# An S4 convolution woven into a SiLU feed-forward: first transform in 64-row halves, the outset in halves, the last step's loads ahead

## The chip, the cores and the metric

The kernel runs on one core of a Trainium2 chip. Its time is the device time of one execution in microseconds (us); several executions are timed, and their median is quoted. One further execution is recorded by the hardware profiler; all durations below come from it. TensorE is PE in the profile (its weight loads PEld), VectorE is DVE, ScalarE is ACT, GpSimd is POOL, and SyncE, which here only issues DMAs, is SP.

## The reference

One sequence of L = 2048 rows with D = 576 channels. Its normalised rows feed two branches, which are added to the input.

```python
xn = layernorm(x)
# branch A: a state-space convolution with N = 128 states a channel
dt = exp(log_dt)[:, None]; A = A_re + 1j*A_im
P  = exp((dt*A)[:, :, None] * arange(L))                 # D x N x L
K  = einsum("dn,dnl,dn->dl", C, P, dt*B).real            # the response
y  = irfft(rfft(pad(xn.T)) * rfft(pad(K)))[:, :L].T + xn * Dskip
# branch B: a feed-forward with F = 4608
out = silu(xn @ w1) @ w2
return x + y + out
```

All inputs and the output are float32.

## The kernel before, in words

**Feed-forward.** `ffn` works on 4 blocks of 512 rows, in two halves of two blocks, and on 9 chunks of 512 hidden units (FT = 4 tiles of 128). Each fp32 operand is split into a high and a low part of a shorter format (fp32r: `h1`, `l1`, `h2`, `l2`, `gh`, `gl`, `xh`, `xl`), and products are taken as high x high + high x low + low x high. `up(blk, t)` (line 255) makes one 128 x 512 tile of hidden units in PSUM with 14 matmuls, applies SiLU (line 268, `gf`), and splits the result on ScalarE (line 269, `gh`) and VectorE (line 270, `gl`). `down(blk, jj)` (line 273) multiplies the gate by w2 for one tile of 128 rows, in two column halves of 12 matmuls (line 285, `po`), and adds to `acc[j]` (line 288). `load_w1` and `load_w2` fetch two tiles of weights at a time into `w1r` and `w2r`, one buffer each, and split them (lines 236, 238, 249, 251).

**Rows.** `phase0` loads two tiles of 128 rows of x, normalises them (`norm`) and transposes them on PE (`put_xt`, lines 114 to 124) into `xh`, `xl`, `x4`. Tiles 0 to 7 are transposed before the woven part, in pool `pa`; tiles 8 to 15 during it, parked in DRAM (`dxt`). All normalised rows also go to DRAM (`dxn`).

**Convolution.** It is a transform of length 2048 by steps of 32 and 64. `spread` does the first step for the rows (line 145, `pu`) into DRAM `d1u`. `kgen` (line 427) makes the response 8 channels and two groups at a time, 36 chunks: sines and magnitudes on ScalarE and VectorE, then per pair of chunks 64 small matmuls over the states (line 530, `kp`, 128 x 32 weights, four column tiles). `kp` is copied to SBUF in two halves (line 539, `kt`), each half is multiplied by the constant `f1` (line 542, `z`: the response's first transform), and `z` is copied into `stage` (line 547), which is stored to DRAM `d1k` every four chunks. `spectral` (line 560) takes 32 frequencies one after another: loads `ur`, `kr`, splits them, second step (`pk`, `pu2`), product, inverse step (`pb`), and stores `yo` to DRAM `d2`. The last step is `add_conv(j, dst)` (line 631): it loads `ys`, 128 x 4 x 288, in two DMAs from `d2`, runs 8 matmuls with 64 rows and 32 columns (line 645, `py`), two row halves and four column tiles, and adds the result to `dst` (line 651). For tiles 8 to 15 `dst` is the accumulator, in `down` of the last chunk (line 278). Tiles 0 to 7 were finished in the first half and put into DRAM `dr0`; `tail` (line 603) reloads each as `r0`, calls `add_conv` and stores it.

**What sets the order.** `weave` (line 31) runs the feed-forward as the main line of 288 steps and resumes `side` when the step reaches a mark. `marks` (line 655) gives the places: response from 0.14 to 0.65, spectral part to 0.88, tail to 0.94. This gives a program order; a list scheduler with its own model of time then moves instructions on each engine, `tc.high_priority()` lifts those inside it, and `behind(ins)` keeps an instruction after another one. What results is a fixed order on each engine, and each engine and each DMA queue works through its own in order. SP's queue holds nearly all loads and stores; POOL's a few. Small PSUM tiles (`pt`, `pu`, `kp`, `z`, `pk`, `pb`, `py`) share three buffers (pool `pss`).

Of the kernel before, what the change touches and what calls it, by code (L numbers as in the profile page):

```python
# [17 lines left out]
P = 128  # L18
# [23 lines left out]
def kernel(  # L42
# [43 lines left out]
    ident = cst.tile([P, P], F32, name="ident")  # L86
    f1 = cst.tile([P, 2 * P], F32, name="f1")
    s4 = None
# [37 lines left out]
    xts = {}  # L126
    pins = {}

    def spread(up):
# [86 lines left out]

    def behind(ins):
        return tc.issue_after(ins) if ins is not None else nullcontext()

    def ffn():  # L220
# [4 lines left out]
        def load_w1(half, c, t):  # L225
            f = c * FT + t
            r1 = wp.tile([P, 5, 2 * P], F32, tag="w1r", name="w1r", bufs=1)
            fs = slice(f * P, (f + 2) * P)
            nc.sync.dma_start(r1[:, 0:4, :], w1[0:512, fs].rearrange("(k p) f -> p k f", p=P))
            nc.sync.dma_start(r1[0:64, 4, :], w1[512:576, fs])  # L230
            nc.sync.dma_start(r1[64:128, 4, :], w1[512:576, fs])
            for i in range(2):
                h1 = wp.tile([P, 5, P], F32R, tag="w1h", name="w1h", bufs=FT + 1)
                l1 = wp.tile([P, 5, P], F32R, tag="w1l", name="w1l", bufs=FT + 1)
                src = r1[:, :, i * P:(i + 1) * P]
                nc.scalar.copy(h1, src)  # L236
                with behind(pins["xt_v"] if f == half == 0 else None):
                    nc.vector.tensor_sub(l1, src, h1)  # L238
                W1[half, c, t + i] = h1, l1

        def load_w2(half, c, t):
            f = c * FT + t
            r2 = wp.tile([P, 2, D], F32, tag="w2r", name="w2r", bufs=1)
            nc.sync.dma_start(r2, w2v[:, f:f + 2, :])
            for i in range(2):
                h2 = wp.tile([P, D], F32R, tag="w2h", name="w2h", bufs=FT + 1)
                l2 = wp.tile([P, D], F32R, tag="w2l", name="w2l", bufs=FT + 1)
                with behind(pins["xt_s"] if f == half == 0 else None):
                    nc.scalar.copy(h2, r2[:, i, :])  # L249
                with behind(pins["xt_v"] if f == half == 0 else None):  # L250
                    nc.vector.tensor_sub(l2, r2[:, i, :], h2)  # L251
                W2[half, c, t + i] = h2, l2
                yield

        def up(blk, t):
            half, c, b = blk
            xh, xl, x4 = xts[2 * half + b]
            h1, l1 = W1[half, c, t]
            ph = ps1.tile([P, 512], F32, tag="ps1", name="ph")
# [3 lines left out]
            nc.tensor.matmul(ph, h1[:, 4, :], x4, start=False, stop=False)  # L263
            nc.tensor.matmul(ph, l1[:, 4, :], x4, start=False, stop=True)  # L264
            gf = gp.tile([P, 512], F32, tag="gf", name="gf", bufs=2)
            gh = gp.tile([P, 512], F32R, tag="gh", name="gh")
            gl = gp.tile([P, 512], F32R, tag="gl", name="gl")
# [3 lines left out]
            G[blk, t] = gh, gl  # L271

        def down(blk, jj):
            half, c, b = blk
            j = 8 * half + 4 * b + jj
            js = slice(jj * P, (jj + 1) * P)
            if half == 1 and c == NCH - 1:
                add_conv(j, acc[j])
            for h in range(2):
                hs = slice(h * HD, (h + 1) * HD)  # L280
                po = ps2.tile([P, 512], F32, tag="ps2", name="po")
                n = 0
                for t in range(FT):
                    for g, w in ((0, 0), (0, 1), (1, 0)):
                        nc.tensor.matmul(po[:, :HD], G[blk, t][g][:, js], W2[half, c, t][w][:, hs],  # L285
                                         start=n == 0, stop=n == 3 * FT - 1)
# [51 lines left out]

    kl = yp = None
    kf = {}  # L340
# [86 lines left out]
    def kgen():  # L427
        lrT, fT, rhoT, phiT = (kf[n] for n in ("lr", "f", "rho", "phi"))
        with tc.tile_pool(name="kg", bufs=1) as kg:
# [52 lines left out]
            for i in range(NCK):  # L482
# [52 lines left out]
                tabs = []  # L535
                for e in range(2):
                    es = slice(e * 256, (e + 1) * 256)
                    kt = kg.tile([P, 256], F32, tag="kt", name="kt", bufs=2)
                    nc.scalar.copy(kt, kp[:, es])
                    z = pss.tile([P, 512], F32, tag="pss", name="z")  # L540
                    for gl in range(2):
                        nc.tensor.matmul(z[:, gl * 256:(gl + 1) * 256], kt[:, gl * P:(gl + 1) * P], f1,  # L542
                                         start=True, stop=True)
                    r = (i - 1 + e) % NRUN
                    if r == 0:
                        stage = kg.tile([P, 64, NRUN * CH], F32, tag="stage", name="stage")
                    nc.scalar.copy(
                        stage[:, :, r * CH:(r + 1) * CH].rearrange("p k (g c) -> p g k c", g=2),
                        z.rearrange("p (g k c) -> p g k c", g=2, c=4))
                if r == NRUN - 1:  # L550
                    d0 = (i // NRUN) * NRUN * CH
# [51 lines left out]
    def tail():  # L603
        for j in range(8):
            r0 = yp.tile([P, D], F32, tag="r0", name="r0")
            nc.sync.dma_start(r0, dr0[j * P:(j + 1) * P, :])
            add_conv(j, r0)
            store(r0, j, (nc.sync,))
            yield 2 + (j + 1) / 8

# [12 lines left out]
    def mm3(dst, terms, hs):  # L623

        n = 0
        for sh, sl, (mh, ml) in terms:
            for st, mv in ((sh, mh), (sh, ml), (sl, mh)):
                nc.tensor.matmul(dst, st, mv[:, hs], start=n == 0, stop=n == 3 * len(terms) - 1)  # L628
                n += 1

    def add_conv(j, dst):

        ys = yp.tile([P, 4, HD], F32, tag="ys", name="ys")
        for h in range(2):
            nc.sync.dma_start(ys[64 * h:64 * h + 64],
                              d2[j * 256:(j + 1) * 256, h * HD:(h + 1) * HD].rearrange("(q r) d -> r q d", q=4))
        first = None
        py = [pss.tile([P, 512], F32, tag="pss", name="py") for _ in range(2)]
        for q1 in range(2):
            for q2 in range(2):  # L640
                for h in (1, 0):
                    o = 64 * q1 + 32 * q2
                    rows = slice(64 * h, 64 * h + 64)
                    with tc.high_priority(), behind(first):
                        mm = nc.tensor.matmul(py[h][o:o + 32, :HD], s4[rows], ys[rows, 2 * q2 + q1],
                                              start=True, stop=True,
                                              tile_position=(64 * h, o), skip_group_check=True)
                    first = first or mm.ins
        for h in range(2):
# [3 lines left out]
    def side():  # L653
        nonlocal s4, kl, yp
        marks = (0.14, 0.65, 0.88, 0.94)
        with tc.tile_pool(name="pa", bufs=4) as pa:
            for js in ((0, 1), (2, 3), (4, 5), (6, 7)):
                phase0(pa, js)
                if js[0] == 2:
# [30 lines left out]
        def at_mark(at):  # L690
            k = int(at)
            return marks[k] + (at - k) * (marks[k + 1] - marks[k]) if k < 3 else marks[3]

# [27 lines left out]
def _constants():  # L721
# [9 lines left out]
    for q in range(4):  # L731
        f1[q, :, :, :, q] = cs
    s4 = np.broadcast_to(cs.transpose(2, 1, 0) / L, (2, 2, 32, 32)).reshape(P, 32)
    s1 = np.stack(_hi_lo(s1.reshape(P, P)), 1)
    f1 = f1.reshape(P, 256)
    n2 = np.arange(64)
# [51 lines left out]
```

## Time and profile before

| | |
|---|---|
| median of 3 runs | 1187.77 us (1185.72 to 1189.12) |
| profiled execution, own time | 1184.91 us |
| its span, first to last instruction | 1183.1 us |
| granted TensorE clock, mean | 0.987 |
| z matmuls (line 542) | 144 records, median 379 ns |
| py matmuls (line 645) | 256 records, median 427 ns |
| ys loads (line 635) | 32 of 288 KB, median 5.6 us to landing |
| w1r loads | 36 of 512 KB, median 4.7 us to landing |
| idle ScalarE until a w1r load (line 236) | 64.8 us in 24 times, longest 7.5 us |
| idle PE until a ys load | 14.6 us in 6 times, longest 7.7 us |

How to read it: a matmul's record lasts from its start until its modelled end, and matmuls overlap in the array, so the time that one takes of PE is the distance from its start to the next start. An fp32 matmul leaves two records. "Idle before, releaser" names what ended a wait. DMAs are listed with the time from issue to landing. The granted clock (PEclk) is the share of full speed that the throttle gave TensorE.

### The profile page before, as it was taken

The page shows a single profiled execution, that of the slowest core. Times are in us where ns is not written, and L with a number is a line of the kernel's source. Part 1 is how long each engine was busy: PE and PEld are TensorE (multiplying, and loading weights), DVE is VectorE, ACT ScalarE, POOL GpSimd, SP SyncE. Part 2 cuts the span into 40 slices and gives each one's busy share as a digit, 9 for nine tenths or more (in the row PEclk, how much of TensorE's full clock was granted, in tenths as well). Part 3 has the DMA queues.
Part 4 walks back from the last instruction along what each step waited for, and adds up shares of the span by engine and source line. Part 5 has one row for each costly group of instructions (what it writes and reads, how often), then busy time and mean ns, then how long its engine had stood idle before and what let it go on. Part 6 is the DMA issues. An engine that isn't in the chain of part 4 may idle for free.

```text
span 1183.1 us, 22598 instructions
## 1 busy us (share of the span) xinstructions
PE 1132.1 (96%) x8984; PEld 1014.9 (86%) x8984; DVE 942.5 (80%) x1645; ACT 699.0 (59%) x1246; POOL 24.7 (2%) x42
## 2 busy tenths in 40 slices
PE   5999999999999999999999999999999999999958
PEld 3898889888888898998898889899989999999726
DVE  5798898999888989999899985488767878876223
ACT  3465556566565657665665654477767777776200
POOL 1100000000000000000000000000000000000000
PEclk9999999999999999999999999999999999999969
DMA  9356220505124242447451413654544544440895
GB/s 266 117 158 202 78 85 21 132 31 120 62 84 89 93 89 93 89 155 211 153 132 47 124 47 94 167 165 145 151 128 146 154 142 145 151 148 31 214 245 132
DMA packets 161625, 148.92 MB, mean 126 GB/s; under 512 B 82448, under 2 KB 124192, under 8 KB 161008
## 3 DMA queue, kind: packets, MB, share of 16 engines
q1 hardware_dynamic: 157088, 132.19, 39.7%
q0 software_dynamic: 3472, 13.53, 4.0%
q10 hardware_dynamic: 960, 1.77, 0.6%
q8 instruction: 70, 1.15, 0.4%
q14 instruction: 35, 0.29, 0.1%
HBM read 102.63 MB, written 44.90 MB: 125 GB/s over the span
## 4 chain that ended last, share of the span: by engine, by line
PE 65%; DMA 12%; DVE 11%; ACT 6%; issue 3%; SPq 2%; POOL 0%; ACTq 0%; DVEq 0%; POOLq 0%
PE po L285 27%; PE ph L262 23%; DMA w1r<-in_B_w_dram 3%; DMA d1u<-u 2%; PE kp L530 2%; DMA ys<-d 2%; PE pk L628 2%; PE pb L628 2%; PE pu L628 2%; PE z L542 2%; PE ph L263 2%; PE ph L264 2%; DVE acc L288 1%; DVE S L509 1%; DVE C L509 1%
## 5 line engine op out<-in xcount | busy, mean ns | idle before, releaser
L285 PE MATMUL po<-w2h,gh 128*128 128x288 f32 x1152 | 337.7, 299 | 6.8 <-ACT gh L269 5.9
L285 PE MATMUL po<-w2l,gh 128*128 128x288 f32 x1152 | 339.6, 297 | 0.4 <-issue 0.4
L285 PE MATMUL po<-w2h,gl 128*128 128x288 f32 x1152 | 333.9, 297 | 1.4 <-DVE gl L270 1.4
L285 PEld LDWEIGHTS po<-w2h,gh 128*128 128x128 f32 x1152 | 216.5, 189 | 16.9 <-ACT gh L269 6.8
L285 PEld LDWEIGHTS po<-w2l,gh 128*128 128x128 f32 x1152 | 217.8, 189 | 6.4 <-issue 2.0
L285 PEld LDWEIGHTS po<-w2h,gl 128*128 128x128 f32 x1152 | 215.7, 189 | 4.9 <-DVE gl L270 2.2
L262 PE MATMUL ph<-xh,w1h 128*128 128x512 f32 x576 | 161.6, 396 | 4.7 <-ACT gf L268 2.7
L262 PE MATMUL ph<-xl,w1h 128*128 128x512 f32 x576 | 160.2, 391 | 0.0
L262 PE MATMUL ph<-xh,w1l 128*128 128x512 f32 x576 | 159.8, 392 | 0.0
L288 DVE TENSOR_TENSOR acc<-po,acc 128x288 f32<-128x288 f32 x288 | 125.6, 451 | 28.4 <-PE po L285 27.1
L262 PEld LDWEIGHTS ph<-xh,w1l 128*128 128x128 f32 x576 | 107.0, 188 | 22.3 <-issue 1.4
L268 ACT ACTIVATE gf<-ph 128x512 f32<-128x512 f32 x144 | 85.7, 596 | 68.2 <-PE ph L264 43.9
L262 PEld LDWEIGHTS ph<-xl,w1h 128*128 128x128 f32 x576 | 106.7, 188 | 20.7
L262 PEld LDWEIGHTS ph<-xh,w1h 128*128 128x128 f32 x576 | 104.2, 189 | 23.2 <-ACT gf L268 3.7
L269 ACT CAST gh<-gf 128x512 fp32r<-128x512 f32 x144 | 88.1, 620 | 48.5 <-PE po L285 46.6
L270 DVE TENSOR_TENSOR gl<-gf,gh 128x512 fp32r<-128x512 f32 x144 | 97.9, 684 | 18.0 <-ACT gh L269 17.2
L236 ACT CAST w1h<-w1r 128x640 fp32r<-128x640 f32 x72 | 51.6, 724 | 72.6 <-DMA w1r<-in_B_w_dram 64.8
L238 DVE TENSOR_TENSOR w1l<-w1r,w1h 128x640 fp32r<-128x640 f32 x72 | 58.7, 820 | 25.1 <-ACT w1h L236 24.8
L249 ACT CAST w2h<-w2r 128x576 fp32r<-128x576 f32 x72 | 46.5, 672 | 26.3 <-DMA w2r<-in_B_w_dram 21.5
L251 DVE TENSOR_TENSOR w2l<-w2r,w2h 128x576 fp32r<-128x576 f32 x72 | 52.6, 751 | 8.9 <-ACT w2h L249 8.5
L489 ACT ACTIVATE c<-th,magic 128x1040 f32<-128x1040 f32 x36 | 41.9, 1165 | 29.9 <-DVE C L510 22.0
L264 PE MATMUL ph<-x,w1l 128*128 128x512 f32 x144 | 56.6, 393 | 0.0
(169 smaller groups left out, 1845.2 us busy)
## 6 DMA issues: line engine op xcount, KB each, us to landing
w2r<-in_B_w_dram SPq DMA_DIRECT2D x36, 576.0 KB, 3.9
w1r<-in_B_w_dram SPq DMA_DIRECT2D x36, 512.0 KB, 4.7
d1u<-u SPq DMA_DIRECT2D x32, 288.0 KB, 2.6
d1k<-stage SPq DMA_DIRECT2D x18, 512.0 KB, 8.0
ur<-d1u SPq DMA_DIRECT2D x32, 288.0 KB, 3.7
kr<-d1k SPq DMA_DIRECT2D x32, 288.0 KB, 2.9
d<-yo SPq DMA_DIRECT2D x32, 288.0 KB, 3.9
ys<-d SPq DMA_DIRECT2D x32, 288.0 KB, 5.6
```

The costliest lines, as they stand in the source:

```text
L236: nc.scalar.copy(h1, src)
L238: nc.vector.tensor_sub(l1, src, h1)
L249: nc.scalar.copy(h2, r2[:, i, :])
L251: nc.vector.tensor_sub(l2, r2[:, i, :], h2)
L262: nc.tensor.matmul(ph, w[:, kt, :], v[:, kt, :], start=n + kt == 0, stop=False)
L264: nc.tensor.matmul(ph, l1[:, 4, :], x4, start=False, stop=True)
L268: nc.scalar.activation(gf, ph, AF.Silu)
L269: nc.scalar.copy(gh, gf)
L270: pins["gl"] = nc.vector.tensor_sub(gl, gf, gh).ins
L285: nc.tensor.matmul(po[:, :HD], G[blk, t][g][:, js], W2[half, c, t][w][:, hs], start=n == 0, stop=n == 3 * FT - 1)
L288: nc.vector.tensor_add(acc[j][:, hs], po[:, :HD], acc[j][:, hs])
L628: nc.tensor.matmul(dst, st, mv[:, hs], start=n == 0, stop=n == 3 * len(terms) - 1)
```

## The change

It has three parts.

1. **Response's first transform.** `f1` shrinks from 128 x 256 to 128 x 128: two groups of 64 rows for four of 32, each acting for two channels instead of four. `kp` is copied in one piece. Instead of four matmuls with 128 rows and 256 columns a pair of chunks has eight with 64 rows and 128 columns: rows 0 to 63 (array position 0) into one PSUM tile, rows 64 to 127 (position 64) into another, in turn, with high priority. The copies into `stage` become two strided ones of 512 elements.
2. **The outset.** For the first chunk the second pair of weight tiles gets buffers of its own (`w1r`, `w2r` in pool `pa`), the first `w1r` is loaded by POOL's queue, both w1 loads are written ahead of both w2 loads, and the splits on VectorE and ScalarE are put behind other points. The first block's `up` runs in two column halves of 256: all four tiles of hidden units for the first 256 rows, then for the others. Tiles 4 to 7 of x come behind the transposition of tile 3 (`behind(pins["xt3"] ...)` stands for the last two pairs).
3. **The last step.** `conv_load` fetches `ys` (four buffers for three) two tiles ahead of `add_conv`, `tail_load` the reloaded `r0`; `py` loses its high priority and is put behind the latest feed-forward matmul (`pins["pe"]`). The marks move: spectral part to 0.875, the tail from 0.905 to 0.945.

The diff, cut to its core:

```diff
         def load_w1(half, c, t):
             f = c * FT + t
-            r1 = wp.tile([P, 5, 2 * P], F32, tag="w1r", name="w1r", bufs=1)
+            first = half == 0 and f < FT
+            r1 = (pa if first and t else wp).tile([P, 5, 2 * P], F32, tag="w1r", name="w1r", bufs=1)
...
+            eng = nc.gpsimd if first and t == 0 else nc.sync
+            eng.dma_start(r1[:, 0:4, :], w1[0:512, fs].rearrange("(k p) f -> p k f", p=P))
...
-                with behind(pins["xt_v"] if f == half == 0 else None):
-                    nc.vector.tensor_sub(l1, src, h1)
+                with behind(pins["xt1"] if first else None):
+                    pins["w1l"] = nc.vector.tensor_sub(l1, src, h1).ins
...
-        def up(blk, t):
+        def up(blk, t, a=0, e=512):
...
-                    nc.tensor.matmul(ph, w[:, kt, :], v[:, kt, :], start=n + kt == 0, stop=False)
+                    nc.tensor.matmul(ph, w[:, kt, :], v[:, kt, a:e], start=n + kt == 0, stop=False)
...
             if half == 1 and c == NCH - 1:
+                conv_load(j + 2)
                 add_conv(j, acc[j])
...
         for t in (0, 2):
             load_w1(0, 0, t)
+        for t in (0, 2):
             for _ in load_w2(0, 0, t):
                 pass
         yield 0
         for t in range(FT):
-            up(blocks[0], t)
+            up(blocks[0], t, 0, 256)
+        for t in range(FT):
+            up(blocks[0], t, 256, 512)
             yield 3.0
...
-                for e in range(2):
-                    es = slice(e * 256, (e + 1) * 256)
-                    kt = kg.tile([P, 256], F32, tag="kt", name="kt", bufs=2)
-                    nc.scalar.copy(kt, kp[:, es])
-                    z = pss.tile([P, 512], F32, tag="pss", name="z")
-                    for gl in range(2):
-                        nc.tensor.matmul(z[:, gl * 256:(gl + 1) * 256], kt[:, gl * P:(gl + 1) * P], f1,
-                                         start=True, stop=True)
+                kt = kg.tile([P, 512], F32, tag="kt", name="kt")
+                nc.scalar.copy(kt, kp)
+                z = [pss.tile([P, 512], F32, tag="pss", name="z") for _ in range(2)]
+                first = None
+                for eg in range(4):
+                    for h in (1, 0):
+                        rows = slice(64 * h, 64 * h + 64)
+                        with tc.high_priority(), behind(first):
+                            mm = nc.tensor.matmul(z[h][:, eg * P:(eg + 1) * P], kt[rows, eg * P:(eg + 1) * P], f1[rows],
+                                                  start=True, stop=True, tile_position=(64 * h, 0))
+                        first = first or mm.ins
...
     def tail():
         for j in range(8):
-            r0 = yp.tile([P, D], F32, tag="r0", name="r0")
-            nc.sync.dma_start(r0, dr0[j * P:(j + 1) * P, :])
-            add_conv(j, r0)
-            store(r0, j, (nc.sync,))
-            yield 2 + (j + 1) / 8
+            if j < 2:
+                conv_load(j)
+                r0s[j] = tail_load(j)
+        for j in range(8):
+            yield 3 + j / 8
+            if j < 6:
+                r0s[j + 2] = tail_load(j + 2)
+            conv_load(j + 2)
+            add_conv(j, r0s[j])
+            store(r0s[j], j, (nc.sync,))
...
+    def conv_load(j):
+        if j < NJ:
+            yss[j] = yp.tile([P, 4, HD], F32, tag="ys", name="ys", bufs=4)
+            for h in range(2):
+                nc.sync.dma_start(yss[j][64 * h:64 * h + 64],
+                                  d2[j * 256:(j + 1) * 256, h * HD:(h + 1) * HD].rearrange("(q r) d -> r q d", q=4))
...
-        first = None
+        first = pins["pe"]
...
-        marks = (0.14, 0.65, 0.88, 0.94)
+        marks = (0.14, 0.65, 0.875, 0.905, 0.945)
...
-    f1 = np.zeros((4, 32, 32, 2, 4), f8)
+    f1 = np.zeros((2, 2, 32, 32, 2, 2), f8)
```

More of the change, by code (lines that the diff above doesn't have):

```diff
@@ L86 @@
     ident = cst.tile([P, P], F32, name="ident")
-    f1 = cst.tile([P, 2 * P], F32, name="f1")
+    f1 = cst.tile([P, P], F32, name="f1")
     s4 = None
@@ L127, with behind @@
     pins = {}
+    def behind(ins):
+        return tc.issue_after(ins) if ins is not None else nullcontext()
     def spread(up):
@@ L242, in load_w2 @@
             f = c * FT + t
-            r2 = wp.tile([P, 2, D], F32, tag="w2r", name="w2r", bufs=1)
+            first = half == 0 and f < FT
+            r2 = (pa if first and t else wp).tile([P, 2, D], F32, tag="w2r", name="w2r", bufs=1)
             nc.sync.dma_start(r2, w2v[:, f:f + 2, :])
@@ L247, in load_w2 @@
                 l2 = wp.tile([P, D], F32R, tag="w2l", name="w2l", bufs=FT + 1)
-                with behind(pins["xt_s"] if f == half == 0 else None):
+                with behind(pins["xt_s"] if first else None):
                     nc.scalar.copy(h2, r2[:, i, :])
-                with behind(pins["xt_v"] if f == half == 0 else None):
+                with behind(pins["w1l"] if first else None):
                     nc.vector.tensor_sub(l2, r2[:, i, :], h2)
@@ L258, in up @@
             h1, l1 = W1[half, c, t]
-            ph = ps1.tile([P, 512], F32, tag="ps1", name="ph")
+            ph = ps1.tile([P, 512], F32, tag="ps1", name="ph")[:, a:e]
             for n, (w, v) in enumerate(((h1, xh), (h1, xl), (l1, xh))):
                 for kt in range(NKT):
-                    nc.tensor.matmul(ph, w[:, kt, :], v[:, kt, :], start=n + kt == 0, stop=False)
[L263 to L267, printed above, removed]
+                    nc.tensor.matmul(ph, w[:, kt, :], v[:, kt, a:e], start=n + kt == 0, stop=False)
+            nc.tensor.matmul(ph, h1[:, 4, :], x4[:, a:e], start=False, stop=False)
+            pins["pe"] = nc.tensor.matmul(ph, l1[:, 4, :], x4[:, a:e], start=False, stop=True).ins
+            gf = gp.tile([P, 512], F32, tag="gf", name="gf", bufs=2)[:, a:e]
+            if a == 0:
+                G[blk, t] = [gp.tile([P, 512], F32R, tag=n, name=n) for n in ("gh", "gl")]
+            gh, gl = (g[:, a:e] for g in G[blk, t])
             nc.scalar.activation(gf, ph, AF.Silu)
@@ L284, in down @@
                     for g, w in ((0, 0), (0, 1), (1, 0)):
-                        nc.tensor.matmul(po[:, :HD], G[blk, t][g][:, js], W2[half, c, t][w][:, hs],
-                                         start=n == 0, stop=n == 3 * FT - 1)
+                        pins["pe"] = nc.tensor.matmul(po[:, :HD], G[blk, t][g][:, js], W2[half, c, t][w][:, hs],
+                                                      start=n == 0, stop=n == 3 * FT - 1).ins
                         n += 1
@@ L604, in tail, with tail_load @@
         for j in range(8):
-            r0 = yp.tile([P, D], F32, tag="r0", name="r0")
-            nc.sync.dma_start(r0, dr0[j * P:(j + 1) * P, :])
-            add_conv(j, r0)
-            store(r0, j, (nc.sync,))
-            yield 2 + (j + 1) / 8
+            if j < 2:
[8 more added lines that the diff above has]
+            store(r0s[j], j, (nc.sync,))
+    r0s, yss = {}, {}
+    def tail_load(j):
+        r0 = yp.tile([P, D], F32, tag="r0", name="r0", bufs=3)
+        nc.sync.dma_start(r0, dr0[j * P:(j + 1) * P, :])
+        return r0
     def split_of(t, tag):
@@ L629, in mm3 @@
                 n += 1
-    def add_conv(j, dst):
[L633 to L636, printed above, removed]
-        first = None
-        py = [pss.tile([P, 512], F32, tag="pss", name="py") for _ in range(2)]
[L639 to L648, printed above, removed]
+    def conv_load(j):
+        if j < NJ:
+            yss[j] = yp.tile([P, 4, HD], F32, tag="ys", name="ys", bufs=4)
+            for h in range(2):
+                nc.sync.dma_start(yss[j][64 * h:64 * h + 64],
+                                  d2[j * 256:(j + 1) * 256, h * HD:(h + 1) * HD].rearrange("(q r) d -> r q d", q=4))
+    def add_conv(j, dst):
+        ys = yss.pop(j)
+        py = [pss.tile([P, 512], F32, tag="pss", name="py") for _ in range(2)]
+        first = pins["pe"]
+        for n in range(8):
+            q1, q2, h = n // 4, n // 2 % 2, 1 - n % 2
+            o = 64 * q1 + 32 * q2
+            rows = slice(64 * h, 64 * h + 64)
+            with behind(first):
+                mm = nc.tensor.matmul(py[h][o:o + 32, :HD], s4[rows], ys[rows, 2 * q2 + q1],
+                                      start=True, stop=True, tile_position=(64 * h, o), skip_group_check=True)
+            if n == 0:
+                first = mm.ins
         for h in range(2):
@@ L653, in side @@
     def side():
-        nonlocal s4, kl, yp
-        marks = (0.14, 0.65, 0.88, 0.94)
+        nonlocal s4, kl, yp, pa
+        marks = (0.14, 0.65, 0.875, 0.905, 0.945)
         with tc.tile_pool(name="pa", bufs=4) as pa:
             for js in ((0, 1), (2, 3), (4, 5), (6, 7)):
-                phase0(pa, js)
+                with behind(pins["xt3"] if js[0] > 2 else None):
+                    phase0(pa, js)
+                pins[f"xt{js[1]}"] = pins["xt_v"]
                 if js[0] == 2:
@@ L727, in _constants @@
     s1 = np.zeros((2, 2, 32, 32, 2, 2), f8)
[L728 removed]
+    f1 = np.zeros((2, 2, 32, 32, 2, 2), f8)
     for q in range(2):
         s1[:, q, :, :, :, q] = cs
[L731 to L732 removed]
+        f1[:, q, :, :, :, q] = cs
     s4 = np.broadcast_to(cs.transpose(2, 1, 0) / L, (2, 2, 32, 32)).reshape(P, 32)
     s1 = np.stack(_hi_lo(s1.reshape(P, P)), 1)
[L735 removed]
+    f1 = f1.reshape(P, P)
     n2 = np.arange(64)
```

25 lines of the change are left out of this document (10 added, 15 removed).

## The prediction

> **What bounds the kernel now.** I read the page's busy rows first. In the first block below TensorE (PE) is busy for 96% of the span, and the second rows cut the span into 40 slices: PE stands at 9 everywhere but in the first slice and the last two, and the granted clock (PEclk) falls only at the end.
>
> ```profile
> PE 1132.1 (96%) x8984; PEld 1014.9 (86%) x8984; DVE 942.5 (80%) x1645; ACT 699.0 (59%) x1246; POOL 24.7 (2%) x42
> ...
> PE   5999999999999999999999999999999999999958
> PEclk9999999999999999999999999999999999999969
> DMA  9356220505124242447451413654544544440895
> ```
>
> So a microsecond is won in three ways: idle PE at the start, PE work taken out of the middle, idle PE at the end. The busy time by stretches sizes them (columns: stretch, its length, PE, PEld, DVE, ACT, POOL busy, clock, DMA share, GB/s):
>
> ```profile
> 0.00:40.00 40.00, 25.38 (x119) 19.87 (x120) 24.55 (x64) 18.92 (x36) 4.11 (x10) 1.00 0.82 244
> 150.00:750.00 600.00, 591.26 (x5534) 532.69 (x5533) 532.87 (x836) 360.55 (x562) 5.70 (x10) 1.00 0.37 98
> 1096.00:1124.00 28.00, 26.79 (x181) 20.64 (x181) 7.22 (x14) 7.24 (x12) 0.00 (x0) 1.00 0.85 211
> 1124.00:1152.00 28.00, 15.04 (x136) 7.17 (x134) 6.91 (x17) 0.00 (x0) 0.00 (x0) 0.63 0.99 244
> ```
>
> The start leaves 14.6 us of PE idle, the middle 8.7 us in 600. In the last row PE is busy 15.0 of 28 us at a clock of 0.63, while the DMA engines are at 0.99: there the transfers set the pace. The chain of waits agrees; between 1097 and 1160 us it runs through ys loads, stores and SP's issues:
>
> ```profile
> 1100.08 8.03 DMA r<-dr
> 1108.13 5.32 DMA out_dram<-r
> ...
> 1137.98 0.43 SPq L606
> 1138.51 0.58 SPq L635
> 1139.13 0.61 SPq L635
> 1139.84 0.57 SPq L635
> 1140.47 6.06 DMA ys<-d
> ```
>
> **Step 1: the response's first transform (z).** Now, per pair of chunks, 4 matmuls with 128 rows and 256 columns; fp32 runs each as two records. One group in order of time:
>
> ```profile
> 180.63 0.29 PE L285 MATMUL po<-w2h,gl 128*128 128x288 f32 x1
> 180.76 1.89 PE L542 MATMUL z<-f,kt 128*128 128x256 f32 x8
> 182.30 0.48 PE L145 MATMUL pu<-sp,s 128*128 128x288 f32 x1
> 182.62 0.30 PE L146 MATMUL pu<-sp,s 128*128 128x288 f32 x1
> ```
>
> From 180.76 to 182.30, plus 0.19 by which the next gap (0.32) exceeds the usual 0.13, is 1.73 us, or 0.216 us a record. 18 pairs make 31 us of PE. Afterwards a pair has 8 matmuls (16 records) of 128 columns, half the length, so 0.108 us each: 1.73 us if they ran one after another, 0.86 us if the two 64-row halves run beside each other. That they can is shown by the convolution's last step, which already uses 64-row halves (with 32 columns):
>
> ```profile
> 1113.93 0.43 PE L285 MATMUL po<-w2h,gl 128*128 128x288 f32 x2
> 1114.29 0.72 PE L645 MATMUL py<-ys,s 64*32 64x288 f32 x16
> 1114.93 0.40 PE L285 MATMUL po<-w2h,gh 128*128 128x288 f32 x1
> 1115.17 0.29 PE L285 MATMUL po<-w2l,gh 128*128 128x288 f32 x1
> ```
>
> 16 records of 288 columns would be 16 x 0.243 = 3.9 us in a row (0.216 x 288/256); the group takes 0.64 us, which 8 tiles two records deep (0.49 us) explain and four do not. The rest, 0.15 us, plus 0.11 us on the next gap (0.24 for 0.13), is the price of going into and out of a split array: 0.26 us. The new group is then 0.86 + 0.26 = 1.12 us; saved are 0.61 us a pair, 11 us in 18. Bounds: 0.86 us a pair without the price (15 us), and a loss of 0.26 us a pair (4.7 us) if the halves do not overlap. PE is at 98.5% between 150 and 750 us, so I count nine tenths or less: **-9.5 us**. DVE is at 89% there and can follow.
>
> The Trainium skill, page TensorEngine Tiling (Array Packing), section Key Properties, says that a change of the tiling mode drains TensorE, which speaks against two more changes per pair; the 0.26 us above is that price in this trace.
>
> The rest costs nothing: the copies of kt go from two of 0.373 us to one of 0.57 us or so (a 512-element copy of z takes 0.586), the stage copies keep 36 x 512 elements, d1k's stores keep size and number. z now takes two of the three small PSUM buffers at once, so the pu matmuls behind it wait for its ScalarE copies; in the issue order of the changed kernel 2 pu follow at once and the next after some 20 matmuls (2.6 us), against two copies of 0.586. Only a late kt would stop the queue (rival D).
>
> **Step 2: the outset.** Now one w1r and one w2r buffer serve both weight pairs. The second w1r load is issued at 21.89 us, when VectorE has read the first, and lands at 27.47 (its issue plus the chain's 4.59 us from 22.88); PE stands from 26.2 to 28.3. The up matmuls start only at 17.64 us, with all four 128-row blocks of x transposed. Afterwards all four weight loads go out at once (the first by POOL), and the first gate needs two blocks. I walked the new order with rows of the page: xn at 8.3 us rather than 10.07 (it stands ahead of the next tile's statistics on VectorE now), four w1h casts (0.725 each) on ScalarE, the second xh at about 14.3, so the first up matmuls at 14.5. Then VectorE is late: four w1l (0.82 each), two xl (0.69), eight statistics (0.4 each), w2l (0.75) put the first w2l at about 25 us and the last half gate at about 30. At 32.8 us I have 17.3 us of PE work done (98 up matmuls of 0.118, on the line through 0.132 us for 288 and 0.227 for 512 columns; 27 down of 0.132; 4 transposed blocks of 0.54), so 15.5 us lost. The old kernel at 39.4 us had done 21.8 (56 x 0.227, 36 x 0.132, 8 x 0.54), so 17.6 lost. **-2 us**, with bounds of +2 (the loads of x tiles 4 to 7 now stand behind 1.18 MB of w2, and VectorE's statistics behind them) and -5 (the loss up to 14.5 us, about 12.9, stays, and none comes after it). It includes 0.5 us for 112 half matmuls at 0.118 rather than 0.1135.
>
> **Step 3: the end.** The order of PE changes: the inverse transforms (pb) now end with 64.3 us of matmul work left rather than 58.5 (counts times 0.227, 0.132 and 0.08 for py), and the py groups are spread over what remains instead of standing together (six tiles within 5 us of PE work now). py loses its priority and stands in a place fixed by hand; ys has four buffers, two tiles ahead. But SP's queue stays: each of the 288 KB r0 reloads from the fourth on waits for a store to land, and ys loads stand behind it. So I take it as limited by transfers. Now, from the first reload (1096.5) to tile 8's py (1144.3), 33 pieces of 0.295 MB moved: 9.73 MB in 47.8 us, 204 GB/s. With 54.5 us of PE work left at the start and PE's end at 1179.2, 28 us are lost. Afterwards tile 8's ys has 32 pieces and one w2r of 0.59 MB ahead of or in it: 10.0 MB, 49 us at that rate. It begins with 60.3 us of work left (4 us after the last pb, as now) and tile 8 stands where 30.6 are left, so PE ends at 49 + 30.6 = 80 us after the start, 19 lost: **-9 us**. At 250 GB/s, as in the saturated stretches, tile 8 has its data after 40 us: -18 us. Eight more py groups (21 for 13, up to 0.26 us each: 2 us) hide in these waits. From the other side: -2 us if the rate falls to 180, since waits for stores leave the engines empty.
>
> **Sum.** The profiled execution took 1184.9 us (span 1183.1 and 1.8 around it). 1184.9 - 9.5 - 2 - 9 = 1164.4. The median of the runs shown (1187.8) is 2.9 us above that execution, so I predict 1167.3, rounded to 1167.
>
> **Rivals.**
> A, the halves of z do not run side by side, and the first edit does not do what it says. Each half needs a weight load of its own, 16 a pair for 8. The transposes, whose weights are 128 columns, go off every 0.108 us (4 in 0.43 us at 25.25); if weight loads are that long and queue up, a group takes 16 x 0.108 + 0.26 = 1.99 us, 0.26 more than now. The 11 us become a loss of 4.7: 1167 + 9.5 + 4.7 = 1181. For it: no row here shows two loads of 128 columns into two halves at once. Against it: py's 16 loads (0.106 each) all fit into 0.64 us. The Trainium skill, page TensorE: Matmul & The Clock Gate, section LDWEIGHTS, states the rule behind it: a load's time goes by columns, not rows, so half the rows load no faster. Chance 0.15.
>
> B, the tail runs at the saturated rate: 1158. For it: in 1140 to 1152 the engines move about 265 GB/s; against it: SP's waits on landings. Chance 0.10.
>
> C, the transfers take the tail's gain: the rate falls to 170 GB/s, tile 8 comes at 59 us, and PE ends 90 us after the start with the old 28 to 29 lost: 1176. For it: five reloads wait for stores just ahead of them in SP's queue, and a store here took 5.32 us to land. Chance 0.08.
>
> D, slower. z has high priority and stands in PE's in-order queue; if kt's copy is late, everything behind it waits. ScalarE runs phase activations of 1.165 us there; a copy behind two of them comes 2.3 us late. If that happens at each pair for 1.7 us, 31 us are lost: 1198. It turns the sign from 1.1 us a pair (20.5 us in 18). Against it: z follows kp by about 24 matmuls (3 us), and now PE waits for kt twice, 1.1 us in all. Chance 0.05.
>
> **Numbers.** The forecast has 0.62, its own range 1159 to 1175. With A and B the range is 1152 to 1181. A measurement of this kernel tells 0.3% (3.6 us) from no change: faster takes the forecast, B, C and most of A, 0.88; A's upper part and shifts elsewhere give 0.05 within; D and mishaps of A give 0.07 slower.
>
> **What would show it.** z: 288 records, a group from its first record to the next instruction about 1.1 us; near 2 us proves A. Start: first up matmul near 14.5 us and no w1r wait after 20 us. End: last pb earlier against the end by about 6 us of work, PE idle after 1090 us smaller, no stretch at half clock as long as now; the py waits that remain should name ys behind r0 reloads. I am wrong if PE waits for kt at z, or if the loads of the next chunk's weights, which now come after x tiles 8 to 11 on SP, are late near 60 us.

## The result, and the profile after

The changed kernel takes 1169.65 us (median of four runs, 1167.4 to 1173.59) against 1187.86 for the kernel before beside it: ratio 0.9862, 95% interval 0.9833 to 0.989. A second measurement, told below, gave 0.9874 (0.9848 to 0.9899). The forecast was 1167. The profiled execution took 1167.4 us, 17.5 less than that of before.

The page of the changed kernel: busy time, then PE, granted clock and DMA in 40 slices.

```profile
PE 1127.0 (97%) x9184; PEld 1008.3 (87%) x9184; DVE 941.2 (81%) x1649; ACT 701.2 (60%) x1236; POOL 26.1 (2%) x45
...
PE   6999989999999999999999999999999999999888
PEclk9999989999999999999999999999999999999989
DMA  8456120424223341447542323645535554350895
```

The end is nearly whole: 8 8 8 for 9 5 8, clock 9 8 9 for 9 6 9. But there is an 8 that was not there before, in slice 6 (146 to 175 us), in PE and in the clock. The busy times by stretch answer to those of before (stretch, length, PE, PEld, DVE, ACT, POOL, clock, DMA share, GB/s):

```profile
0.00:40.00 40.00, 29.06 (x202) 27.82 (x203) 27.75 (x74) 21.73 (x46) 6.21 (x13) 1.00 0.67 215
142.00:166.00 24.00, 20.63 (x95) 17.23 (x94) 23.96 (x42) 13.36 (x21) 0.00 (x0) 0.86 0.24 74
1096.00:1124.00 28.00, 22.98 (x160) 15.43 (x158) 8.17 (x17) 4.10 (x7) 0.00 (x0) 0.88 0.88 232
1124.00:1152.00 28.00, 26.61 (x227) 19.85 (x227) 11.69 (x26) 3.56 (x6) 0.00 (x0) 1.00 0.86 225
```

PE is busy 29.06 us of the first 40 for 25.38, and 26.61 us of the last stretch for 15.04 at a clock of 1.00 for 0.63. In 142 to 166 us VectorE has 40 ns to spare. In the kernel before, PE was busy through all of that stretch at full clock, and VectorE for 22.85 us of it already:

```profile
142.00:166.00 24.00, 24.00 (x125) 20.74 (x125) 22.85 (x41) 14.75 (x23) 0.00 (x0) 1.00 0.25 78
```

To say where the time went, I compare each matmul's start with the sum of what all matmuls before it cost on PE when nothing holds them up (0.227 us for 512 columns, 0.118 for 256, 0.132 for 288, 0.108 a transposed block, 1.73 or 1.28 us a group of z). The difference is time lost to waits and to a low clock. This table has it for the profiled execution of every kernel with several runs, in us by stretch, with the ratio to the kernel before and its interval:

| kernel | 0 to 60 us | to first z | to last z | to last pb | to PE's end | ratio |
|---|---|---|---|---|---|---|
| before | 20.3 | 3.4 | 19.7 | 10.5 | 27.2 | 1 |
| after | 15.9 | 10.4 | 15.7 | 9.9 | 19.6 | 0.9862 (0.9833 to 0.9890) |
| after, again | 14.8 | 10.1 | 13.6 | 10.9 | 21.1 | 0.9874 (0.9848 to 0.9899) |
| z alone | 19.7 | 4.4 | 26.8 | 9.6 | 25.0 | 0.9939 (0.9918 to 0.9960) |
| outset alone | 15.2 | 9.4 | 18.0 | 8.9 | 26.6 | 0.9948 (0.9928 to 0.9968) |
| last step alone | 20.7 | 3.5 | 19.9 | 9.0 | 23.9 | 0.9965 (0.9941 to 0.9990) |
| z and last step | 20.4 | 3.8 | 24.8 | 8.7 | 20.6 | 0.9903 (0.9871 to 0.9934) |
| r0 in eight buffers | 15.2 | 9.3 | 13.6 | 11.2 | 19.7 | 0.9830 (0.9801 to 0.9859) |
| r0 mostly not reloaded | 14.8 | 9.3 | 15.6 | 12.0 | 15.8 | 0.9806 (0.9777 to 0.9834) |
| response behind addition | 15.0 | 4.1 | 16.8 | 13.8 | 20.2 | 0.9841 (0.9811 to 0.9871) |
| addition first | 14.6 | 9.4 | 13.0 | 6.7 | 20.9 | 0.9787 (0.9761 to 0.9813) |

From before to after, losses fall by 9.6 us (4.4 at the outset, 7.6 at the end, 4.6 in between, and 7.0 more up to the first z), and the nominal work by 7.6 (8.1 for z, less 0.5 for the half matmuls): 17.2 us at PE's end. Each row is one execution, and several lie off their kernel's median: before by up to 3.0 us below it, the changed kernel by 2.2 and 4.2 below, z alone and the outset alone by 2.1 and 2.3 above. So a difference of 3 us between the sums of two rows can be that alone.

### The profile page after: what moved, and what is told of

Its sections match the earlier page's. It is cut to its first block, busy times and chain, and to the rows that moved or that the text cites. A ratio compares the mean times of both kernels' runs of the same rounds, so it can differ in the third digit from the quotient of the medians.

```text
span 1165.6 us, 23033 instructions
## 1 busy us (share of the span) xinstructions
PE 1127.0 (97%) x9184; PEld 1008.3 (87%) x9184; DVE 941.2 (81%) x1649; ACT 701.2 (60%) x1236; POOL 26.1 (2%) x45
## 3 DMA queue, kind: packets, MB, share of 16 engines
q10 hardware_dynamic: 960, 1.77, 0.6%
## 4 chain that ended last, share of the span: by engine, by line
PE 60%; DVE 14%; DMA 11%; ACT 8%; issue 4%; SPq 1%; DVEq 0%; ACTq 0%; POOLq 0%
PE po L290 26%; PE ph L266 21%; DMA w1r<-in_B_w_dram 3%; DMA w2r<-in_B_w_dram 3%; PE kp L539 2%; PE ph L267 2%; PE ph L268 2%; DMA ys<-d 2%; DVE acc L293 1%; PE pb L653 1%; DVE C L507 1%; PE pk L653 1%; PE z L554 1%; DVE w2l L254 1%; PE pu L653 1%
## 5 line engine op out<-in xcount | busy, mean ns | idle before, releaser
L266 PE MATMUL ph<-xh,w1h 128*128 128x512 f32 (+1 forms) x592 | 164.9, 392 | 0.7 <-ACT gf L273 0.7
L266 PE MATMUL ph<-xl,w1h 128*128 128x512 f32 (+1 forms) x592 | 162.9, 390 | 0.0
L266 PE MATMUL ph<-xh,w1l 128*128 128x512 f32 (+1 forms) x592 | 159.9, 388 | 0.0
L273 ACT ACTIVATE gf<-ph 128x512 f32<-128x512 f32 (+1 forms) x148 | 86.3, 583 | 87.7 <-PE ph L268 53.9
L266 PEld LDWEIGHTS ph<-xh,w1l 128*128 128x128 f32 x592 | 109.4, 190 | 21.7 <-issue 0.9
L266 PEld LDWEIGHTS ph<-xl,w1h 128*128 128x128 f32 x592 | 109.3, 191 | 21.4 <-issue 0.9
L275 DVE TENSOR_TENSOR gl<-gf,gh 128x512 fp32r<-128x512 f32 (+1 forms) x148 | 97.9, 670 | 18.1 <-ACT gh L274 16.3
L274 ACT CAST gh<-gf 128x512 fp32r<-128x512 f32 (+1 forms) x148 | 88.6, 608 | 34.2 <-PE po L290 20.6
L500 ACT ACTIVATE c<-th 128x1040 f32<-128x1040 f32 x36 | 38.7, 1075 | 41.5 <-DVE th L499 41.5
L498 ACT ACTIVATE c<-th,magic 128x1040 f32<-128x1040 f32 x36 | 42.0, 1166 | 26.4 <-DVE C L519 19.9
```

The costliest lines, as they stand in the source:

```text
L266: nc.tensor.matmul(ph, w[:, kt, :], v[:, kt, a:e], start=n + kt == 0, stop=False)
L498: nc.scalar.activation(c65, th, AF.Identity, bias=magic)
L500: nc.scalar.activation(c65, th, AF.Abs)
```

## The experiments

**One part at a time.** The edits are the parts 1, 2 and 3 of the change, each alone with all that belongs to it, and then 1 with 3 (the changed kernel without the outset). One line of each, of z, the outset and the last step:

```diff
+                                                  start=True, stop=True, tile_position=(64 * h, 0))
...
+            up(blocks[0], t, 0, 256)
...
+                conv_load(j + 2)
```

> The kernel before with the first edit alone: z on two 64-row halves. Theory (halves overlap, a group costs 1.29 us for 1.73, as in the trace after): 18 x 0.44 = 8 us less, a ratio near 0.993, and no half-clock stretch more than before. Rival (the gain of z goes into other waits of PE, since VectorE is busy 89% of that stretch): under 3 us less, and PE's idle time between 180 and 700 us grows by 5 us or more.

> The second edit alone: second weight buffers and the first gates in halves. First up matmul near 14.3 us, and about 4 us less of PE lost by 60 us. Theory (an early start is given back where VectorE is bound): near 150 us PE stands for VectorE and a stretch of half clock follows, so that the end is 0 to 2 us earlier, ratio 0.998 to 1.000. Rival (nothing takes it back): 4 us less, ratio 0.9966, and no pause near 150 us.

> The third edit alone: ys loads two tiles ahead, the inverse transforms earlier, py in a fixed place. Theory (the tail's loss goes from 27 to 20 us whatever comes before it): 8 us less, ratio 0.9935. Rival (what moved the tail was the earlier arrival of all the work before it): 3 us less or none.

> The changed kernel without its second edit. If the three edits add up and the outset's gain lasts, this takes 4 us more than the changed kernel (1173 to 1174, ratio 0.988). Theory (the outset's gain is given back near 150 us): within 2 us of the changed kernel (ratio 0.985 to 0.988), with no pause of PE for VectorE near 150 us and no half-clock stretch at 152 us.

With the before of those runs at 1186.07 us, z alone saves 7.2 us (4.7 to 9.7), the outset 6.2 (3.8 to 8.5), the last step 4.2 (1.2 to 7.0), z and the last step 11.5 (7.8 to 15.3). Together the parts add up to 17.6, and the whole change has 15 to 16.4. So z's theory has the right size. My theory of the outset falls: I said that the pause near 150 us would eat its gain, and in the trace the pause is there (9.4 us lost from 60 us to the first z), yet the kernel gains 6 us. Beside the other two parts (the table's z and last step, against the whole change) it gains 4.5 us at the start, loses 6.6 up to the first z and gains 9.1 up to the last. The last step is worth about half of what I expected: its interval leaves out my 8 us and holds the rival's 3. Its own trace has 3.3 us less lost behind the last pb, with z beside it 6.6; why the end gains more in company is open.

z alone shows something else: between first and last z it loses 26.8 us for 19.7, with three stretches of 6.83 us at half clock for one of 3.41. So what its theory said of half clock falls, and the rival's second clause is right, though its first (under 3 us less) is not. The waits of PE in that kernel from 505 to 575 us (total, times, longest) and the instructions behind the first of them:

```profile
PE po L286 <- DVE acc L289: 3.6, 1, 3.6
PE po L286 <- ACT w2h L249: 3.4, 1, 3.4
```

```profile
513.12 0.54 POOL L299 DMA_DIRECT2D xl<-dxt  x1 [373.45 <-PE ph L263]
514.02 0.53 POOL L298 DMA_DIRECT2D xh<-dxt  x1 [0.37 <-PE ph L263]
514.09 0.38 SPq L244 DMA_DIRECT2D w2r<-in_B_w_dram  x1
...
522.56 1.24 ACT L249 CAST w2h<-w2r 128x576 fp32r<-128x576 f32 x2 [5.35 <-DMA w2r<-in_B_w_dram]
...
523.29 1.09 PE L286 MATMUL po<-w2h,gh 128*128 128x288 f32 x3 [3.43 <-ACT w2h L249]
```

At the change of halves, x for the next half (2.4 MB) and the next w2r start within 1.5 us. The w2r load takes 8.1 us or more until ScalarE has it (median on its page 3.9), and PE stands 3.43 us. The order on PE moved: when xl is fetched, 1536 down matmuls have been issued and 11 pairs of chunks, 1476 and 10 in the kernel before. A pause of this kind is in all kernels with the new z and the old outset (also at 564 us), in none of the table's kernels with all three parts. Of the kernels with all three parts that follow below, it is in two (each z matmul twice, and the halves not in turn), which have 1536 and 11 as well. But the one with z by halves has these counts too, its w2r starts 0.6 us after xh and takes 8.9 us to land, and PE has no such pause. So the counts alone don't make it; that the order does is read from the traces and not shown by a run that forces it.

**What a group of z is made of.** First each z matmul twice:

```diff
                         with tc.high_priority(), behind(first):
+                            for _ in range(2):
...
```

> The changed kernel with each z matmul issued twice in a row (same values): 32 records a pair for 16. It tells how the 1.29 us of a group is made up. The halves overlap and going in and out of the split array costs a fixed 0.43 us (0.054 us a record): 32 x 0.054 + 0.43 = 2.16 us. The price is 0.26 us as with py and each record takes longer, 0.0645 us: 32 x 0.0645 + 0.26 = 2.32 us. No fixed price, all of it by records: 2.58 us. No overlap at all (0.108 us a record): 3.5 us or more.

A group in the changed kernel, and in this one:

```profile
182.43 1.16 PE L554 MATMUL z<-f,kt 64*128 64x128 f32 x16
183.52 0.40 PE L290 MATMUL po<-w2l,gh 128*128 128x288 f32 x1
183.76 0.29 PE L290 MATMUL po<-w2h,gl 128*128 128x288 f32 x1
```

```profile
180.00 2.16 PE L555 MATMUL z<-f,kt 64*128 64x128 f32 x32
182.09 0.40 PE L290 MATMUL po<-w2l,gh 128*128 128x288 f32 x1
```

From the group's first start to the next instruction it is 1.09 us in the one, 2.09 in the other. With the longer gaps ahead of it and behind it (0.09 and 0.11 us in both) a group costs 1.29 and 2.29 us. Of the four sums, 2.32 (a price of 0.26 us, longer records) is nearest to that, but the single starts in the trace say otherwise. In the changed kernel two records start 6 ns apart, one in each half, and a new pair starts every 0.112 us; only the first pair takes 0.214, and the last is followed after 0.208. So the overlap is full, 8 slots of 0.112 = 0.89 us, and 0.40 us is a fixed price: 0.10 at the first pair, 0.10 behind the last, 0.09 ahead, 0.11 on the next gap. Doubled, the order was not strictly in turn and 17 slots were needed: 17 x 0.112 + 0.40 = 2.30. The whole kernel took 1198.23 us in its one run, 13 us above before.

Then the order of the halves:

```diff
-  for eg in range(4):
-      for h in (1, 0):
+  for h in (1, 0):
+      for eg in range(4):
```

> The changed kernel with the four z matmuls of rows 64 to 127 first and those of rows 0 to 63 behind them, not in turn. Theory (PE starts matmuls in order, and the halves run beside each other only where neighbours use different halves): 14 to 16 records at 0.108 us and a price of 0.26 to 0.43 us, so 1.8 to 2.2 us a group for 1.29. Rival (the second half's matmuls start while the first half's still run, whatever the order): 1.3 us a group.

This did not tell it: the scheduler put the halves 1 1 0 1 0 1 0 0 on TensorE, nearly in turn, with 1.39 us a group, one slot more than in turn. (Its one run took 1163.19 us; at 516 us it had a pause like that of z alone.) With each z matmul tied to the one before (`first = mm.ins`):

> The changed kernel with each z matmul put behind the one before, first the four of rows 64 to 127, then the four of rows 0 to 63, so that neighbours in TensorE's order use the same half (in the run with the same wish but without this force, the order on TensorE was 1 1 0 1 0 1 0 0, nearly in turn). Theory (halves run beside each other only as neighbours in the order): 14 to 16 slots of 0.108 us and a price of 0.43 us, 1.9 to 2.2 us a group for 1.29, so slower than the old form's 1.73. Rival (the second half's matmuls start while the first half's run): about 1.3 us.

```profile
181.88 1.71 PE L554 MATMUL z<-f,kt 64*128 64x128 f32 x16
183.52 0.40 PE L290 MATMUL po<-w2l,gh 128*128 128x288 f32 x1
```

1.64 us to the next instruction, 1.84 with the gaps, between theory and rival. The starts show four records alone, then slots with two records and with one (the fifth, seventh and eighth have two, the sixth one), then five alone: 13 slots, and 13 x 0.112 + 0.40 = 1.86. So PE starts the second half beside the last four records of the first, no earlier. In turn is what makes the group 1.29; by halves it is slower than the old form's 1.73. The kernel's time does not show it: its one run took 1167.12 us, no more than the changed kernel, though its groups cost 18 x 0.55 = 9.9 us more. Its order on PE is another from 188 us on, and its other losses are smaller; a group's cost is read from the trace, not from one such time.

**What the end waits for.** First the reloads' buffers:

```diff
-        r0 = yp.tile([P, D], F32, tag="r0", name="r0", bufs=3)
+        r0 = yp.tile([P, D], F32, tag="r0", name="r0", bufs=8)
```

> The changed kernel with eight buffers for r0, so that no reload waits for a store to land; ys still has four. Theory (the five reloads behind stores on SP's queue hold the ys loads back): SP's waits for landed stores of r (4.5 us) go, PE's waits for ys (4.6 us) mostly go, 3 to 4 us less than the changed kernel, ratio to the kernel before near 0.983. Rival (the transfers themselves set the pace, 225 to 265 GB/s from 1096 to 1144 us): the reloads only move ahead of ys loads, and the time is the same within 1.5 us, ratio 0.985 to 0.988.

PE's waits from the last pb to the end, in the changed kernel and in this one:

```profile
PE py L673 <- DMA ys<-d: 4.6, 4, 1.6
PE py L673 <- DVE r L679: 3.6, 3, 1.6
```

```profile
PE py L673 <- DMA ys<-d: 7.7, 6, 3.2
PE py L673 <- DVE r L679: 0.6, 1, 0.6
```

SP's waits of its reloads for stores (4.5 us in 7) are gone, and PE waits 8.3 us for 8.2: for ys rather than for the additions. The loss behind the last pb is 19.7 us for 19.6. The trace is on the rival's side; the ratio 0.983 lies nearer to the theory, but its interval overlaps both measurements of the changed kernel. Then fewer bytes:

```diff
+        if j < 2:
             nc.sync.dma_start(r0, dr0[j * P:(j + 1) * P, :])
+        else:
+            nc.gpsimd.memset(r0, 0.0)
```

> The changed kernel with eight buffers for r0, and six of the eight reloads of r0 left out (the buffer is set to zero by GpSimd, so the feed-forward's part is missing from six tiles of the output): 6 x 295 KB = 1.77 MB less to move in the tail, no other wait added. Theory (the tail's transfers set its pace at about 250 GB/s): 7 us less work for the engines, 4 to 7 us less loss after the last pb (13 to 16 us for 19.7), ratio to the kernel before 0.977 to 0.980. Rival (order and waits in SP's queue set the pace, not the bytes): loss after the last pb stays at 18 to 20 us, ratio 0.982 to 0.985.

With 1.77 MB less, 15.8 us are lost behind the last pb for 19.7: 3.9 us, about half of what these bytes take at 250 GB/s. It holds only for the trace: the ratios of the two (0.9806, 0.983) overlap. So by the traces the bytes are a good part of what limits the end, and waits of SP for stores are not. Two things stay open. The six loads also left SP's queue, where issuing one takes 0.34 to 0.6 us, and this run does not tell that from the bytes. And by the ratios eight buffers are 4 to 5 us below the changed kernel, which the end of their trace does not show.

**The pause near 150 us.** In the changed kernel (VectorE's instructions, then PE's):

```profile
147.68 1.22 DVE L507 TENSOR_TENSOR C<-pw 128x1024 f32<-128x1024 f32 x1
148.82 0.69 DVE L503 TENSOR_TENSOR C<-pw,al 128x512 f32<-128x512 f32 x1
149.42 1.22 DVE L507 TENSOR_TENSOR C<-pw 128x1024 f32<-128x1024 f32 x1
150.56 0.69 DVE L503 TENSOR_TENSOR C<-pw,al 128x512 f32<-128x512 f32 x1
151.16 0.95 DVE L468 RECIPROCAL md<-md 128x128 f32<-128x128 f32 x1
152.02 0.40 DVE L293 TENSOR_TENSOR acc<-po,acc 128x288 f32<-128x288 f32 x1
```

```profile
152.47 0.42 PE L290 MATMUL po<-w2h,gh 128*128 128x288 f32 x1 [2.45 <-DVE acc L293]
```

PE needs the PSUM buffer that the addition at 152.02 reads; five instructions of the response stand ahead of it in VectorE's order. After the pause TensorE runs at half clock from 152.71 for 6.83 us. Two edits:

```diff
+                with tc.high_priority():
                     nc.vector.tensor_add(acc[j][:, hs], po[:, :HD], acc[j][:, hs])
```

> The changed kernel with the addition of po to acc on VectorE at high priority. In the trace after, that addition stands behind 4.7 us of the response's work on VectorE at 147.3 to 152.0 us; PE waits 2.45 us for it, and 6.83 us at half clock follow. Theory (it is this place in VectorE's order that gives the outset's gain back): no such pause, 60 us to the first z with about 3 us lost for 10, and 4 to 6 us less than the changed kernel, ratio to the kernel before 0.981 to 0.983. Rival (VectorE has no free time there, so another of its results is late for PE instead): the loss up to the first z stays at 8 to 10 us, and the ratio at 0.985 to 0.988.

```diff
+                pins["acc"] = nc.vector.tensor_add(acc[j][:, hs], po[:, :HD], acc[j][:, hs]).ins
...
+                with behind(pins["acc"] if i < 2 else None):
                     nc.vector.tensor_mul(
...
+                with behind(pins["acc"] if i == 2 else None):
                     nc.vector.reciprocal(md, md)
```

> The changed kernel with three of VectorE's instructions for the response's second and third chunk (the two magnitude products of 1.22 and 0.69 us and a reciprocal of 0.95) put behind the latest addition of po to acc, so that the addition which came at 152.0 us has 2.6 to 2.9 us less ahead of it. Theory (the half-clock stretch of 6.83 us follows the pause of 2.45 us): the pause shrinks to under 0.5 us, no half-clock stretch near 152 us, loss from 60 us to the first z 3 to 5 us for 10, and 5 us less than the changed kernel, ratio to the kernel before about 0.982. Rival (the half clock at about 150 us comes without the pause too, or another late result of VectorE replaces it): the loss to the first z stays at 8 to 10 us, ratio 0.985 to 0.988.

The priority did not move that addition at all: pause and half clock stay (9.4 us up to the first z), so it did not test the theory. It changed the order only in the last quarter, where 6.7 us are lost between last z and last pb for 9.9 to 12.0 in the four that share its order up to there; and it is the fastest of all, 0.9787, with an interval below both measurements of the changed kernel. The second edit does test it. From 142 to 166 us:

```profile
142.00:166.00 24.00, 22.76 (x124) 19.55 (x123) 20.62 (x35) 17.07 (x24) 0.00 (x0) 1.00 0.32 104
```

PE is busy 22.76 us for 20.63, the clock is 1.00 for 0.86, and 4.1 us are lost up to the first z for 10.4. So the pause and the half clock hang on the place of that addition. (The edit moved more than it: the first z comes at 193.6 us for 182.4.) But the kernel gains less than 5 us (0.9841, which overlaps with the changed kernel): the orders behind it differ, and 13.8 us are lost from the last z to the last pb for 9.9.

**The changed kernel again.** The kernels with eight buffers, with few reloads and with the addition first have the changed kernel's order up to 720 us, and still the last z came earlier in them.

> The changed kernel itself once more. Up to about 720 us the order on every engine is the same in it and in the kernels with eight buffers for r0, with zeroed r0 and with the addition at high priority (that one differs from it only after 4600 of TensorE's 6100 rows, in the spectral part), yet the last z starts at 716.9, 718.4 and 715.7 us in those three and at 720.8 us in the first trace of the changed kernel. Theory (the chip's own variation between executions makes that difference, and the edits are worth only what the traces show behind 720 us: 0 us for eight buffers, 2 us for the priority): the ratio to the kernel before comes out at 0.980 to 0.984 here, and the last z at 716 to 719 us. Rival (the first measurement holds, and the priority is worth 9 us): 0.985 to 0.988, the last z near 721 us.

The ratio is the rival's, 0.9874; the last z is the theory's, 717.2 us. So the first trace was a late one up to there, and the changed kernel's 0.987 stands. The priority's gain is in the times; the traces show 3 to 4 us of it from the last z to the last pb, and the rest I can't place.

## Why the prediction was right

The time came within 2.7 us of the forecast's, and its sign and range held. By terms, against the profiled executions:

- **z, -9.5; measured 18 x (1.73 - 1.29) = -7.9.** The mechanism is right, the halves run side by side, and rival A is out. By times z saves 7.2 us alone. What was mis-sized is the price of going in and out, 0.26 us read from py, which is 0.40 here, and a little the slot, 0.112 us for 0.108. The reading of py left out the gap ahead of the group, which there too is 0.22 us for the usual 0.13. The Trainium skill, page TensorEngine Tiling (Array Packing), section Key Properties, says that tiles work independently and that a change of mode drains TensorE; the starts 6 ns apart and the fixed 0.40 us agree with both. Rival D did not come: one wait of z for kt, 1.0 us.
- **Outset, -2; -4.4 at 60 us.** The first up matmul came at 14.30 us (14.5 forecast, 17.64 before). It then lost 7.0 us up to the first z, in a place that the prediction did not look at: it asked for kt and for w1r near 60 us, not what a PE that runs ahead finds on VectorE at 150 us. That VectorE was busy 22.85 of 24 us there before could be read. By times the outset saves 6.2 us alone, three times the forecast. Its sum has a slip: 17.6 less 15.5 counts the half matmuls as work, so the 0.5 us that they cost is not in it, as it says, but comes on top; the -4.4 is counted in the same way.
- **End, -9; -7.6 behind the last pb in the first trace (27.2 to 19.6, foreseen 28 to 19), -6.1 in the second, -4.2 (1.2 to 7.0) as time when done alone.** The order, 21 groups of py for 13, and, in part, transfers as the limit were right. That reloads behind stores hold up ys was the wrong detail, as the trace with eight buffers shows.
- **Not in the sum: 4.6 us less lost between first z and last pb.** With all three parts the order at the change of halves avoids the collision that z alone has, but the kernel before had none there either; its larger losses were a dozen small waits, 4.7 us with half clock from 301 to 311 us the largest, and no single cause for the difference was found. By traces the three misses, -2.4, +7.0 and -4.6, cancel, and the smaller terms z and end leave +1.6 and +1.4: together 3.0 us above the sum of 1164.4, as the 1167.4 of the trace is (the 0.5 us of the half matmuls and roundings cancel). By the times of the parts alone it is of the same kind: the outset saves 4.2 us more than forecast, z 2.3 and the end 4.8 less.

So the result is nearer than the reasons deserve: errors of 4 to 7 us had opposite signs, and that is luck.

## What to carry to other kernels

Give an engine that is the bound an earlier start, and ask at each later place where a second engine is full which of its results comes due sooner; the pause there may cost more than its length. In a kernel whose order a scheduler sets, every edit also draws a new order elsewhere: size this by running parts alone, and compare losses stretch by stretch. Halves of the array pay when neighbours in the order alternate between them and the group is long against a fixed price of 0.4 us.

## What the runs showed of the hardware

- Half clock came in stretches of 3.41, 6.83, 10.24 or 20.48 us only, multiples of 3.41, behind pauses of PE (apart from the one in which each trace ends). In all 14 traces each began a whole number of 3.41 us after the clock first stood at 1.00. The Trainium skill, page TensorE: Matmul & The Clock Gate, section What's actually happening, gives a window of 3413 ns and about one idle window as what lowers the clock. The unit agrees; the idle time does not: 2.45 us at 150 us was enough for 6.83 us in every kernel that had it, and pauses of 0.53 and 1.46 us at 303.6 and 304.8 us for 3.41 in the kernel before. Length alone does not settle it: a pause of 2.25 us at 737.2 us, in the kernel with the response behind the addition, had no half clock behind it. Whether the place of a pause among these units decides, no run here shows.
- With the same order on every engine up to there, the last z began at 715.7 to 720.8 us in five traces (one exchange of two instructions on VectorE apart). A difference of 5 us between two traces of such kernels is no evidence by itself.
